# Attention over a key/value cache: tiles of four heads with 64 KiB rows, in three buffers that take turns

## The chip, the cores and the metric

The kernel runs on one core of one Trainium2 chip. The core has five engines with an instruction queue each: PE (TensorE, matrix products), DVE (VectorE), ACT (ScalarE), POOL (GpSimd) and SP (SyncE), which here issues nearly all loads. Loads go from the chip's HBM to SBUF, the on-chip memory of 128 partitions, through 16 DMA engines that all queues share. The metric is the time on the device in microseconds (us), the median of several runs.

## The reference, cut to what matters

One decode step of a transformer layer for two sequences: attention of one new token over a cache of 8192 keys and values, then a small gated network. All inputs are bf16.

```python
B, Sq, D = 2, 1, 512
Hq, Hkv, Sk, Dh = 32, 32, 8192, 128       # k_cache, v_cache: [B, Hkv, Sk, Dh]

def _A_ref(x, k, v, wq, wo):
    q = (x @ wq).reshape(B, Sq, Hq, Dh).transpose(0, 2, 1, 3)
    scores = einsum("bhqd,bhkd->bhqk", q, k) * (Dh ** -0.5)
    p = softmax(scores, axis=-1)
    o = einsum("bhqk,bhkd->bhqd", p, v)
    return o.transpose(0, 2, 1, 3).reshape(B, Sq, Hq * Dh) @ wo

def _B_ref(x, W_gate, W_up, W_down):      # F = 1376
    gate, up = x @ W_gate, x @ W_up
    return (gate * (gate > 0) * up) @ W_down

h = x + _A_ref(layernorm(x), ...)
out = h + _B_ref(layernorm(h), ...)
```

The two caches hold 2 x 2 x 32 x 8192 x 128 bf16 numbers, 268 MB, and each is read once. Each head has its own keys and values, so a key is used for one dot product and a value for one weighted sum.

## The kernel before, in words

**Tiles.** A tile is one sequence and two heads (`NG` = 16 pairs of heads, `steps` has N = 32 tiles). A tile's 2 x 8192 keys are spread over the 128 partitions: 64 partitions for each head (`HALF`), NT = 128 keys in each partition, so a partition's row is 128 x 128 bf16 = 32 KiB (`ROW`). One load of K or of V is 128 such rows, 4 MiB (`load_kv`, L140 to L148). K has two buffers (`kbuf`), V two (`vbuf`), tile i uses number i mod 2. The weights `wq` and later `wo` have a buffer of their own (`wbig`).

**Scores** (`scores`, L320). DVE multiplies the whole K tile by the tile's query in place (L358), the query being repeated over the keys (`qrep`). Then it halves each key's 128 products four times by adding one half to the other (L383: 64, 32, 16, 8 sums), and reduces the last 8 (L387) to the 128 scores of each partition, `scol`. In the last tile PE transposes 16 of the columns and multiplies them by q (L346, L337), and ACT sums 8 columns with its accumulator (L373).

**Softmax.** `pm` is each partition's maximum (L395). A PE product with a constant matrix brings the maxima of all partitions to every partition (`mx_ps`, L397). `powers` (L305) takes each head's extreme from that product on DVE (`nm`, L312), and ACT writes the exponentials to `pgz` (L315), one instruction for each head, with their sums in `zc`.

**Values** (`values`, L414). PE multiplies four columns of exponentials by four keys' values at a time. 32 such matmuls make a tile. Two stand by themselves (L408), 30 run in a hardware loop of two each on PE's sequencer (L438 to L440). The loop is in a block of its own (`tile_critical`, L434), which PE enters by semaphore waits and a branch (recorded at L642). ACT copies the result out (`collect`, L450). After each group of tiles `turn` and `sums` bring the outputs to columns, and `normalise` divides.

**Order of the work.** PE, DVE, ACT and SP run their instructions in the order in which the program lists them. In `scores(i)` the product of tile i comes first, then `powers(i-1)` and `values(i-1)`, then the loads of K(i+1) and V(i) are listed, then the halving of tile i and the PE product for its maximum. So the sequence of loads on SP is wq, K0 in four pieces, K1, V0, and then K(i+1), V(i) for each tile. The last tiles' values are not looped: FRONT of tile N-2 early, the last tile in columns (L420).

**The query** (`make_q`, L231). For each group of 512 columns of `wq`, PE multiplies x by them (L234, four matmuls), ACT copies the row to `qrow` (L238), PE replicates it over the partitions (L242, four matmuls) and ACT copies that to `qrep` (L246). There are eight such groups. Two are made before the first tile, the others one by one behind `scores(0)` to `scores(5)`.

**The end.** Behind the last V come 8.4 MB of weights (`wo`, gate, up, down), into `wbig` and K's first buffer. Then follow the product with `wo` (L535), the layer norm, and the gated network (L571, L604).

Of the kernel before, what the change touches and what calls it, by code (L numbers as in the profile page):

```python
# [23 lines left out]
def kernel(  # L24
# [20 lines left out]
    HALF = P // 2  # L45


    NT = 2 * Sk // P
    ROW = NT * Dh
    NG = Hq // 2  # L50
# [3 lines left out]
    NPE = 16  # L54
    NACT = (0, 8)
# [4 lines left out]
    AGAIN = 8  # L60
# [18 lines left out]

    assert Sq == 1 and Hkv == Hq and Dh == P and D == KC * P and Hq == 32 and B == 2  # L80
# [4 lines left out]
    small = ctx.enter_context(tc.tile_pool(name="small", bufs=2))  # L85
# [4 lines left out]
    pad = big.tile([P, 192], bf16)  # L90
# [3 lines left out]
    wbig = big.tile([P, max(KC * Hq * Dh, sum(rows) * D)], bf16)  # L94
    wd_r = big.tile([P, D], bf16)

    kh = [kbuf[:, s, :] for s in range(2)]
    wq_all = wbig[:, 0:KC * Hq * Dh]
    wq_sb = wq_all.rearrange("p (c n) -> p c n", c=KC)

    wgu = kbuf[:, 0, 0:2 * KC * F].rearrange("p (k c f) -> p k c f", k=2, c=KC)
    wd_sb = kbuf[:, 0, 2 * KC * F:2 * KC * F + FULL * D].rearrange("p (f n) -> p f n", f=FULL)

    qrep = consts.tile([P, B, NG, Dh], bf16)
    qrow = consts.tile([P, Hq * Dh], bf16)
    pgz = [consts.tile([P, NT * 2], bf16, name=f"pgz{s}") for s in range(2)]
    zc = consts.tile([P, B, NG, 2], f32)
# [8 lines left out]
    pick = consts.tile([P, B, HALF], bf16)  # L116
    sel = consts.tile([P, T4, 4, 2], f32)
# [6 lines left out]
    qT = consts.tile([P, 2, B], bf16)  # L124
    xrow = consts.tile([P, D], bf16)
    xc = consts.tile([P, B, KC], f32)
    hc = consts.tile([P, B, KC], f32)

    steps = [(b, g) for b in range(B) for g in range(NG)]
    N = len(steps)  # L130

    COLS = N - 1
    LOOPED = N - 3


    TOGETHER = N - 4

    FRONT = 24

    def load_kv(cache, buf, i, pieces=1):  # L140
        b, g = steps[i]
        w = ROW // pieces
        for k in range(pieces):
            nc.sync.dma_start(  # L144
                out=buf[i % 2][:, k * w:(k + 1) * w],
                in_=_dram(cache, (b * Hkv + 2 * g) * Sk * Dh + k * w, [[ROW, P], [1, w]]),
                single_packet=0 < i < TOGETHER,
            )  # L148

# [14 lines left out]
    with tc.manual_schedule(engines=ORDERED):  # L164

        nc.sync.dma_start(out=wq_all, in_=_dram(A_wq, 0, [[KC * Hq * Dh, P], [1, KC * Hq * Dh]]))  # L166
# [10 lines left out]
        select(pick, 1.0, 0, [[-1, B], [0, HALF]], 1)  # L177
# [3 lines left out]
        for s in range(2):  # L181
            nc.gpsimd.memset(pgz[s], 0.0)
# [14 lines left out]
        for j in range(2):  # L197
            select(sel[:, :, :, j], 1.0, -j, [[-2, T4], [-32, 4]], 1)
# [32 lines left out]
        def make_q(n):  # L231
# [7 lines left out]
            r_ps = ps2.tile([P, B, 2, Dh], f32, tag="tp", name="r_ps")  # L239
            for b in range(B):  # L240
                for j in range(2):
# [4 lines left out]
            nc.scalar.activation(out=qrep[:, :, 2 * n:2 * n + 2, :], in_=r_ps, func=ACT.Copy)  # L246
            if n == NG // 2 - 1:
                qT_ps = ps.tile([P, 2, B], f32, tag="acc")
                for h in range(2):
                    nc.tensor.matmul(  # L250
                        out=qT_ps[:, h, :], lhsT=qrow[0:B, (Hq - 2 + h) * Dh:(Hq - 1 + h) * Dh],
                        rhs=ident[0:B, 0:B], start=True, stop=True,
                    )
# [7 lines left out]
        groups = {}  # L261
        for b in range(B):
            for g0 in range(0, NG, 4):
                if b == B - 1 and g0 + 4 == NG:
                    for g1, n in ((g0, 3), (g0 + 3, 1)):
                        groups[b * NG + g1 + n - 1] = (b, g1, n)
                else:
                    groups[b * NG + g0 + 3] = (b, g0, 4)

        divided = {NG - 1: (0, 0, NG), N - 5: (1, 0, NG - 4), N - 2: groups[N - 2], N - 1: groups[N - 1]}  # L270
# [10 lines left out]
        def o_of(i):  # L281
            key = B if i == N - 1 else steps[i][0]
            if key not in o_ps:
                o_ps[key] = ps2.tile([P, 2, 2 * NG], f32, tag="o", name="o_ps")
            return o_ps[key]

        def sums(i):
            b, g0, n = groups[i]
            nc.tensor.matmul(  # L289
                out=o_of(i)[:, 1, 2 * g0:2 * (g0 + n)], lhsT=ones, rhs=zc[:, b, g0:g0 + n, :], start=True, stop=True,  # L290
            )

        def normalise(i):
            b, g0, n = divided[i]
            c = slice(2 * g0, 2 * (g0 + n))
            rz = small.tile([P, 2 * NG], f32, tag="rz")
# [6 lines left out]
        cols = {}  # L303

        def powers(i):  # L305
            b, g = steps[i]
            s = i % 2
            mx_ps, scol = mx.pop(i)
            if i % AGAIN == 0:
                cols["nm"] = small.tile([P, AGAIN, 2], f32, tag="nm", name="nm")  # L310
            nm = cols["nm"][:, i % AGAIN, :]
            nc.vector.tensor_reduce(out=nm, in_=mx_ps, axis=AXIS.X, op=ALU.min)  # L312
            for j in range(2):
                r = slice(j * HALF, (j + 1) * HALF)
                nc.scalar.activation(  # L315
                    out=_free(pgz[s][r, :], j, [[2, NT]]), in_=scol[r, :], func=ACT.Exp, scale=SCALE,
# [3 lines left out]
        def scores(i):  # L320
            b, g = steps[i]
            s = i % 2
            kt = kbuf[:, s, :]
            npe = NPE if i == N - 1 else 0
            nmul = NT - npe
            nv = nmul - NACT[i == N - 1]

            if i % AGAIN == 0:
                cols["scol"] = small.tile([P, AGAIN, NT], f32, tag="scol", name="scol")
            scol = cols["scol"][:, i % AGAIN, :]  # L330
            if npe:
                sc_ps = ps.tile([P, NPE, 2], f32, tag="sc")
                kT = small.tile([P, NPE * P], bf16, tag="kT")

                def times_q(c0):
                    for t in range(c0, c0 + TPC):
                        nc.tensor.matmul(  # L337
                            out=sc_ps[:, t, :], lhsT=kT[:, t * P:(t + 1) * P], rhs=_free(qT, b, [[B, 2]]),
                            start=True, stop=True,
                        )  # L340

                for c0 in range(0, NPE, TPC):
                    t_ps = ps2.tile([P, TPC, P], bf16, tag="tp")
# [3 lines left out]
                    nc.scalar.activation(  # L347
                        out=kT[:, c0 * P:(c0 + TPC) * P], in_=t_ps.rearrange("p t s -> p (t s)"), func=ACT.Copy,
                    )
                    if c0:  # L350
                        times_q(c0 - TPC)
                times_q(NPE - TPC)
                nc.scalar.activation(out=scol[0:HALF, nmul:NT], in_=sc_ps[0:HALF, :, 0], func=ACT.Copy)
                nc.scalar.activation(out=scol[HALF:P, nmul:NT], in_=sc_ps[HALF:P, :, 1], func=ACT.Copy)

            for t0, n in ([(0, NT // 2), (NT // 2, nmul - NT // 2)] if i == 0 else [(0, nmul)]):
# [19 lines left out]
            if i >= 1:  # L376
                if i < N - 1:
                    collect(i - 1)
# [17 lines left out]
            mx_ps = ps.tile([P, 2, HALF], f32, tag="mx")  # L396
# [5 lines left out]
            if 1 <= i < COLS:  # L402
                turn(i - 1)

        def products(i, u0, u1):
            s = i % 2
            for u in range(u0, u1):
                nc.tensor.matmul(  # L408
                    out=made[i][0:2 * T4, :], lhsT=pgz[s][:, u * 2 * T4:(u + 1) * 2 * T4],
                    rhs=vbuf[s][:, u * T4 * Dh:(u + 1) * T4 * Dh],  # L410
# [3 lines left out]
        def values(i):  # L414
            s = i % 2
            if i >= COLS:
                sums(i)
                g = steps[i][1]
                for t in range(NT):
                    nc.tensor.matmul(  # L420
                        out=o_of(i)[:, 0, 2 * g:2 * g + 2],
                        lhsT=vbuf[s][:, t * Dh:(t + 1) * Dh], rhs=pgz[s][:, 2 * t:2 * t + 2],
                        start=(t == 0), stop=(t == NT - 1),
                    )
                    if t == NT // 2:
                        turn(i - 1)
# [3 lines left out]
            if i >= LOOPED:  # L430
                products(i, 0, FRONT if i == N - 2 else NT // T4)
                return

            with tc.tile_critical(sync_engine=PE):  # L434
# [3 lines left out]
                with nc.Fori(1, NT // T4 // LOOP, 1, engines=[PE], head_slot=at) as w:  # L438
                    for u in range(LOOP):
                        nc.tensor.matmul(  # L440
                            out=made[i][0:2 * T4, :],
# [205 lines left out]
```

## Time and profile before

| | |
|---|---|
| median of 3 runs | 659.24 us (659.11 to 659.24) |
| the profiled execution, first to last instruction (its span) | 657.6 us |
| bytes read from HBM | 281.05 MB |
| DVE busy | 607.9 us (92%) |
| PE busy | 398.7 us (61%) |
| ACT busy | 67.0 us (10%) |
| load queue of SP, share of the DMA engines' time | 99.3% |
| loads of K and of V, 4 MiB each | 64, the first K in four pieces |

The profile is of one further execution. Its page gives the span and no other time for that execution; what a run has around the span is the difference of 1.6 us to the median. The page has the busy time of each engine, the same in 40 slices with the DMA rate, the queues, the chain of work that ended last, and groups of instructions by line. The trace behind the page can be asked for stretches, single instructions and waits. A name such as `kbuf<-kbuf,qrep` says what an instruction writes and reads. SPq and PEq are the sequencers of SP and PE: what they record are loads issued and semaphores waited for.

### The profile page before, as it was taken

The numbers are of one execution on the slowest core, as the hardware profiler recorded it, in microseconds if no ns is written. First come the engines' busy times: TensorE is split into PE (matmuls) and PEld (weight loads), VectorE is DVE, ScalarE is ACT, GpSimd is POOL, SyncE is SP. The second block draws the span as 40 slices with busy tenths as digits, with TensorE's granted clock in tenths as the row PEclk, the third lists the DMA queues.
The fourth block names the chain that finished last, engine by engine and source line by source line (L and its number), as shares of the span: only waits on it lengthen the run. The fifth ranks groups of instructions, "written<-read, shape, count | busy, mean of one in ns | idle before, by whom it ended". The sixth has DMA issues, their size and how long they took to land.

```text
span 657.6 us, 7128 instructions
## 1 busy us (share of the span) xinstructions
PE 398.7 (61%) x1647; PEld 129.5 (20%) x1647; DVE 607.9 (92%) x290; ACT 67.0 (10%) x200; POOL 7.9 (1%) x51
## 2 busy tenths in 40 slices
PE   2127666666676555657666556775556665565496
PEld 1002111211121111211112111121112111121256
DVE  0899999999999999999999999999999999999941
ACT  2110111110000000000000000000000000000220
POOL 4000000000000000000000000000000000000000
PEclk9999788798887777898887789767778876779885
DMA  8999999999999999999999999999999999999997
GB/s 359 439 444 421 442 433 427 444 415 446 427 434 433 427 442 425 440 434 427 440 424 441 429 435 432 429 440 424 440 431 432 438 423 441 432 433 436 425 422 298
DMA packets 11379, 281.26 MB, mean 428 GB/s; under 512 B 1282, under 2 KB 1380, under 8 KB 2020
## 3 DMA queue, kind: packets, MB, share of 16 engines
q1 hardware_dynamic: 11360, 281.06, 99.3%
q8 instruction: 9, 0.15, 0.1%
q14 instruction: 6, 0.05, 0.0%
q10 hardware_dynamic: 4, 0.00, 0.0%
HBM read 281.05 MB, written 0.00 MB: 427 GB/s over the span
## 4 chain that ended last, share of the span: by engine, by line
DVE 61%; DMA 36%; PE 1%; issue 1%; SPq 0%; ACT 0%; DVEq 0%; ACTq 0%
DMA kbuf<-in_A_k_cache_dram 30%; DVE kbuf L358 28%; DVE kbuf L383 27%; DVE scol L387 4%; DMA vbuf<-in_A_v_cache_dram 3%; DMA kbuf<-in_B_W_down_dram 3%; PE po L408 1%; DVE nm L312 1%; DVE pm L395 0%; SPq L144 0%; ACT pgz L315 0%; PE d_ps L604 0%; SPq L166 0%; DVE rz L297 0%; PE y_ps L612 0%
## 5 line engine op out<-in xcount | busy, mean ns | idle before, releaser
L440 PE MATMUL po<-vbuf,pgz 128*8 x870 | 300.1, 443 | 68.0 <-issue 66.7
L358 DVE TENSOR_TENSOR kbuf<-kbuf,qrep 128x16384 bf16<-128x16384 bf16 (+2 forms) x33 | 277.1, 8398 | 10.2 <-DMA kbuf<-in_A_k_cache_dram 9.8
L383 DVE TENSOR_TENSOR kbuf<-kbuf 128x8192 bf16<-128x8192 bf16 (+4 forms) x128 | 274.5, 2144 | 3.3
L440 PEld LDWEIGHTS po<-vbuf,pgz 128*8 x870 | 79.9, 92 | 299.1 <-issue 263.9
L408 PE MATMUL po<-vbuf,pgz 128*8 128x512 bf16 x122 | 47.0, 521 | 135.4 <-PEq L434 111.3
L450 ACT ACTIVATE ob<-po 8x512 f32<-8x512 f32 x31 | 18.2, 586 | 436.5 <-PEq L434 427.3
L387 DVE TENSOR_REDUCE scol<-kbuf 128x128 f32<-128x1024 bf16 (+1 forms) x32 | 38.8, 1214 | 1.2
L315 ACT ACTIVATE pgz<-scol,nm 64x128 bf16<-64x128 f32 x64 | 28.0, 438 | 85.4 <-DVE nm L312 84.5
L397 PE MATMUL mx_ps<-nscale,pm 128*128 128x128 f32 x64 | 15.0, 317 | 29.7 <-DVE pm L395 19.0
L408 PEld LDWEIGHTS po<-vbuf,pgz 128*8 128x8 bf16 x58 | 2.7, 84 | 130.4 <-issue 130.4
L397 PEld LDWEIGHTS mx_ps<-nscale,pm 128*128 128x128 f32 x64 | 9.7, 190 | 39.6 <-issue 19.3
L234 PE MATMUL q_ps<-wbig,xn 128*2 128x512 bf16 x32 | 10.7, 469 | 3.0 <-DMA wbig<-in_A_wq_dram 3.0
L315 ACT ACTIVATION_READ_ACCUMULATOR pgz<-scol,nm 64x1 f32 x64 | 11.7, 184 | 0.0
L312 DVE TENSOR_REDUCE nm<-mx_ps 128x2 f32<-128x128 f32 x32 | 9.1, 284 | 1.4 <-PE mx_ps L397 1.4
L408 PEld LDWEIGHTS <-pgz 128*8 128x8 bf16 x64 | 6.1, 98 | 21.3 <-ACT pgz L315 10.0
L395 DVE TENSOR_REDUCE pm<-scol 128x1 f32<-128x128 f32 x32 | 9.1, 286 | 1.1
L459 PE MATMUL o_ps<-sel,ob 128*128 128x8 f32 (+1 forms) x64 | 8.7, 262 | 0.1
L459 PEld LDWEIGHTS o_ps<-sel,ob 128*128 128x128 f32 x64 | 8.0, 197 | 1.4 <-ACT ob L450 1.2
L215 DVE COPY xc<-x_ps 128x8 f32<-128x8 f32 x1 | 0.2, 167 | 8.4 <-PE x_ps L211 8.4
L238 ACT ACTIVATE qrow<-q_ps 2x512 bf16<-2x512 f32 x8 | 4.7, 587 | 29.5 <-PE q_ps L234 29.5
L242 PE MATMUL r_ps<-qrow,pick 2*64 2x256 bf16 x32 | 3.9, 321 | 5.4 <-ACT qrow L238 5.4
L297 DVE RECIPROCAL rz<-o_ps 128x32 f32<-128x32 f32 (+3 forms) x4 | 1.0, 254 | 5.8 <-PE o_ps L289 4.6
(93 smaller groups left out, 75.5 us busy)
## 6 DMA issues: line engine op xcount, KB each, us to landing
vbuf<-in_A_v_cache_dram SPq DMA_DIRECT2D x32, 4096.0 KB, 23.4
kbuf<-in_A_k_cache_dram SPq DMA_DIRECT2D x31, 4096.0 KB, 19.8
wbig<-in_A_wq_dram SPq DMA_DIRECT2D x1, 4096.0 KB, 12.6
kbuf<-in_A_k_cache_dram SPq DMA_DIRECT2D x4, 1024.0 KB, 17.5
wbig<-in_A_wo_dram SPq DMA_DIRECT2D x1, 2048.0 KB, 24.5
wbig<-in_A_wo_dram SPq DMA_DIRECT2D x2, 1024.0 KB, 26.4
kbuf<-in_B_W_gate_dram SPq DMA_DIRECT2D x1, 1376.0 KB, 31.2
kbuf<-in_B_W_up_dram SPq DMA_DIRECT2D x1, 1376.0 KB
```

The lines of the kernel that those rows point to most:

```text
L234: nc.tensor.matmul(out=q_ps[0:B, :], lhsT=xn[:, c, :], rhs=wq_sb[:, c, n * 512:(n + 1) * 512], start=(c == 0), stop=(c == KC - 1),)
L312: nc.vector.tensor_reduce(out=nm, in_=mx_ps, axis=AXIS.X, op=ALU.min)
L315: nc.scalar.activation(out=_free(pgz[s][r, :], j, [[2, NT]]), in_=scol[r, :], func=ACT.Exp, scale=SCALE, bias=nm[r, j:j + 1], accum_out=zc ...
L358: nc.vector.tensor_tensor(out=kv, in0=kv, in1=_free(qrep, (b * NG + g) * Dh, [[0, n], [1, Dh]]), op=ALU.mult,)
L383: nc.vector.tensor_tensor(out=lo, in0=lo, in1=_free(kt, half, [[Dh, nv], [1, half]]), op=ALU.add,)
L387: nc.vector.tensor_reduce(out=scol[:, 0:nv], in_=_free(kt, 0, [[Dh, nv], [1, 8]]), axis=AXIS.X, op=ALU.add,)
L395: nc.vector.tensor_reduce(out=pm, in_=scol, axis=AXIS.X, op=ALU.max)
L397: nc.tensor.matmul(out=mx_ps.rearrange("p a b -> p (a b)"), lhsT=_free(pm, 0, [[0, P]]), rhs=nscale, start=True, stop=True,)
L408: nc.tensor.matmul(out=made[i][0:2 * T4, :], lhsT=pgz[s][:, u * 2 * T4:(u + 1) * 2 * T4], rhs=vbuf[s][:, u * T4 * Dh:(u + 1) * T4 * Dh], s ...
L440: nc.tensor.matmul(out=made[i][0:2 * T4, :], lhsT=pgz[s][:, bass.ds((w * LOOP + u) * (2 * T4), 2 * T4)], rhs=vbuf[s][:, bass.ds((w * LOOP ...
L450: nc.scalar.activation(out=ob[32 * k:32 * k + 2 * T4, :], in_=made.pop(i)[0:2 * T4, :], func=ACT.Copy,)
L459: nc.tensor.matmul(out=o_of(i)[:, 0, 2 * g0:2 * (g0 + n)], lhsT=ob[:, t * Dh:(t + 1) * Dh], rhs=sel[:, t, 0:n, :], start=(t == 0), stop=(t ...
```

## The change

- A tile is four heads (`H4`) and one sequence. Each head has 32 partitions (`QP`), each partition 256 keys (`NT`), a row is 64 KiB. There are 16 tiles, 16 loads of K and 16 of V of 8 MiB each. K's first load is in four pieces as before, now of 2 MiB, V's last in two.
- Three buffers `buf[0..2]` of 64 KiB for each partition take turns, for K and V alike. V(i) goes to the buffer in which K(i) was (`v_at`, `k_at`), when the scores of tile i are done. K(i+2) goes to the buffer of V(i-1), when that tile's values are done. At the start `wq`, `qrow` and `xrow` lie in `buf[1]`, where V0 goes next. At the end all the weights lie in the last K's buffer.
- The loads are listed after `scores(i)`: V(i), then K(i+2).
- One group of `make_q` is made before the first tile, the seven others behind `scores(0)`. The replication has eight matmuls, one for each sequence and head, of half the width.
- A tile has 64 matmuls of `values` in its loop block, and `powers` four exponentials. There is one `pgz`, one `scol`, one `nm`; the pool `small` has one buffer for each name in place of two.
- ACT sums 32 columns in tiles 0 and 1, 8 in the others, 16 in the last. PE makes 48 columns of the last tile's scores. Tiles 14 and 15 have their values in columns (`COLS`).
- `collect` and `turn` come a tile later, in front of and behind `powers(i-1)` of the next `scores`.
- The loads no longer ask for `single_packet`.

```diff
-    NT = 2 * Sk // P
+    H4 = 4
+    QP = P // H4
+    NT = H4 * Sk // P
...
-    NPE = 16
-    NACT = (0, 8)
+    NPE = 48
...
-    small = ctx.enter_context(tc.tile_pool(name="small", bufs=2))
+    small = ctx.enter_context(tc.tile_pool(name="small", bufs=1))
...
-    kbuf = big.tile([P, 2, ROW], bf16)
-    vbuf = [big.tile([P, ROW], bf16, name=f"vbuf{s}") for s in range(2)]
+    buf = [big.tile([P, ROW], bf16, name=f"buf{s}") for s in range(3)]
...
+    k_at = {i: (i - 2) % 3 if i else 0 for i in range(N)}
+    v_at = {i: k_at[i] if i else 1 for i in range(N)}
+    v_at[N - 1] = v_at[N - 3]
+
+    wq_sb = buf[1][:, 0:KC * Hq * Dh].rearrange("p (c n) -> p c n", c=KC)
+    qrow = buf[1][:, KC * Hq * Dh:KC * Hq * Dh + Hq * Dh]
+    xrow = buf[1][:, (KC + 1) * Hq * Dh:(KC + 1) * Hq * Dh + D]
...
+    tail = buf[k_at[N - 1]]
+    wo_sb = tail[:, 0:NWO]
+    wgu = tail[:, NWO:NWO + NGU].rearrange("p (k c f) -> p k c f", k=2, c=KC)
...
+    COLS = N - 2
+    NACT = {i: 32 if i < 2 else 16 if i == N - 1 else 8 for i in range(N)}
...
-                single_packet=0 < i < TOGETHER,
...
+    def load_k(i, pieces=1):
+        load_kv(A_k_cache, buf[k_at[i]], i, pieces)
+
+    def load_v(i, pieces=1):
+        load_kv(A_v_cache, buf[v_at[i]], i, pieces)
...
-        load_kv(A_k_cache, kh, 0, pieces=4)
-        load_kv(A_k_cache, kh, 1)
-        load_kv(A_v_cache, vbuf, 0)
+        load_k(0, pieces=4)
+        load_k(1)
...
             for b in range(B):
-                for j in range(2):
+                for j in range(H4):
                     nc.tensor.matmul(
-                        out=r_ps[j * HALF:(j + 1) * HALF, b], lhsT=pick[0:B, b, :],
-                        rhs=_free(qrow[0:B, :], (4 * n + j) * Dh, [[2 * Dh, 2], [1, Dh]]), start=True, stop=True,
+                        out=r_ps[j * QP:(j + 1) * QP, b], lhsT=pick[0:B, b, :],
+                        rhs=qrow[0:B, (H4 * n + j) * Dh:(H4 * n + j + 1) * Dh], start=True, stop=True,
                     )
...
-        EARLY = 2
-        for n in range(EARLY):
-            make_q(n)
+        make_q(0)
...
-            left = waiting[:]
+            if i >= 2:
+                collect(i - 2)
             if i >= 1:
                 powers(i - 1)
+            if i >= 2:
+                turn(i - 2)
+            left = waiting[:]
             if i >= 1:
                 values(i - 1)
                 tc.no_sync_barrier()
-                if i < N - 1:
-                    load_kv(A_k_cache, kh, i + 1)
-                    load_kv(A_v_cache, vbuf, i)
...
         for i in range(N - 1):
             scores(i)
-            if i + EARLY < NG // 2:
-                make_q(i + EARLY)
-
-        load_kv(A_v_cache, vbuf, N - 1)
+            if i == 0:
+                for n in range(1, NG):
+                    make_q(n)
+            load_v(i)
+            if i + 2 < N:
+                load_k(i + 2)
+        load_v(N - 1, pieces=2)
+        scores(N - 1)
...
-        scores(N - 1)
-        products(N - 2, FRONT, NT // T4)
+        turn(N - 2)
         powers(N - 1)
-        collect(N - 2)
+        normalise(N - 2)
         values(N - 1)
-        turn(N - 1)
-        while waiting:
-            normalise(waiting.pop(0))
+        normalise(N - 1)
```

More of the change, by code (lines that the diff above doesn't have):

```diff
@@ L59 @@
     PARTS = KC * KC
-    AGAIN = 8
     LOOP = 2
@@ L123, with load_kv @@
     orow = [consts.tile([P, n, B], bf16, name=f"orow{k}") for k, n in enumerate(rows)]
-    qT = consts.tile([P, 2, B], bf16)
-    xrow = consts.tile([P, D], bf16)
+    qT = consts.tile([P, H4, B], bf16)
+    kT = consts.tile([P, TPC * P], bf16)
     xc = consts.tile([P, B, KC], f32)
     hc = consts.tile([P, B, KC], f32)
[L129 to L140, printed above, removed]
+    COLS = N - 2
+    NACT = {i: 32 if i < 2 else 16 if i == N - 1 else 8 for i in range(N)}
+    def load_kv(cache, t, i, pieces=1):
         b, g = steps[i]
@@ L180 @@
         select(nscale, -SCALE, 0, [[-1, P]], 1)
-        for s in range(2):
-            nc.gpsimd.memset(pgz[s], 0.0)
+        nc.gpsimd.memset(pgz, 0.0)
         nc.gpsimd.memset(zc, 0.0)
@@ L254, in make_q @@
                 nc.scalar.activation(out=qT, in_=qT_ps, func=ACT.Copy)
-        EARLY = 2
-        for n in range(EARLY):
-            make_q(n)
[L261 to L270, printed above, removed]
+        make_q(0)
+        groups = {3: (0, 0, 4), 7: (0, 4, 4), 11: (1, 0, 4), 13: (1, 4, 2), 14: (1, 6, 1), 15: (1, 7, 1)}
+        assert NG == 8 and COLS == 14
+        divided = {NG - 1: (0, 0, NG), N - 3: (1, 0, NG - 2), N - 2: groups[N - 2], N - 1: groups[N - 1]}
         o_ps = {}
@@ L301 @@
         mx = {}
-        cols = {}
         def powers(i):
             b, g = steps[i]
-            s = i % 2
             mx_ps, scol = mx.pop(i)
-            if i % AGAIN == 0:
-                cols["nm"] = small.tile([P, AGAIN, 2], f32, tag="nm", name="nm")
-            nm = cols["nm"][:, i % AGAIN, :]
+            nm = small.tile([P, H4], f32, tag="nm")
             nc.vector.tensor_reduce(out=nm, in_=mx_ps, axis=AXIS.X, op=ALU.min)
-            for j in range(2):
-                r = slice(j * HALF, (j + 1) * HALF)
+            for j in range(H4):
+                r = slice(j * QP, (j + 1) * QP)
                 nc.scalar.activation(
-                    out=_free(pgz[s][r, :], j, [[2, NT]]), in_=scol[r, :], func=ACT.Exp, scale=SCALE,
+                    out=_free(pgz[r, :], j, [[H4, NT]]), in_=scol[r, :], func=ACT.Exp, scale=SCALE,
                     bias=nm[r, j:j + 1], accum_out=zc[r, b, g, j:j + 1],
@@ L321, in scores, with transposed @@
             b, g = steps[i]
-            s = i % 2
-            kt = kbuf[:, s, :]
+            kt = buf[k_at[i]]
             npe = NPE if i == N - 1 else 0
             nmul = NT - npe
[L326 to L330, printed above, removed]
+            nv = nmul - NACT[i]
+            scol = small.tile([P, NT], f32, tag="scol")
             if npe:
[L332 to L343, printed above, removed]
+                sc_ps = ps.tile([P, NPE, H4], f32, tag="sc")
+                def transposed(c0):
+                    t_ps = ps2.tile([P, TPC, P], bf16, tag="tp", name="t_ps")
                     for k in range(TPC):
@@ L375, in scores @@
                 )
-            if i >= 1:
-                if i < N - 1:
-                    collect(i - 1)
+            if npe:
+                for j in range(H4):
+                    r = slice(j * QP, (j + 1) * QP)
+                    nc.scalar.activation(out=scol[r, nmul:NT], in_=sc_ps[r, :, j], func=ACT.Copy)
             width = Dh
@@ L516 @@
             for b in range(B):
-                sp = small.tile([P, P], bf16, tag="spread")
+                sp = kT[:, b * P:(b + 1) * P]
                 if blocks is not WHOLE:
```

120 lines of the change are left out of this document (59 added, 61 removed).

## The prediction, made before the result was known

> **What bounds the kernel now.** I read the page's DMA rows and chain first, then the stages, then single waits.
>
> ```profile
> span 657.6 us, 7128 instructions
> ...
> PE 398.7 (61%) x1647; PEld 129.5 (20%) x1647; DVE 607.9 (92%) x290; ACT 67.0 (10%) x200; POOL 7.9 (1%) x51
> ...
> q1 hardware_dynamic: 11360, 281.06, 99.3%
> ...
> DVE 61%; DMA 36%; PE 1%; issue 1%; SPq 0%; ACT 0%; DVEq 0%; ACTq 0%
> ```
> The chain names DVE first, yet the load queue is busy for 99.3% of the span. The stages settle it (columns: engines' busy time, granted clock, DMA share, GB/s):
>
> ```profile
> 100.00:200.00 100.00, 65.84 (x221) 20.12 (x220) 99.15 (x43) 12.98 (x37) 0.00 (x0) 0.84 1.00 431
> ...
> 400.00:500.00 100.00, 62.27 (x187) 18.22 (x188) 97.38 (x44) 7.85 (x25) 0.00 (x0) 0.80 1.00 433
> 500.00:600.00 100.00, 62.88 (x198) 18.99 (x197) 98.13 (x43) 7.85 (x25) 0.00 (x0) 0.81 1.00 433
> ```
> The rate is flat at about 433 GB/s. 281.06 MB at 433 take 649 us of the 657.6, so DMA bounds the kernel. DVE follows closely behind it. Any gap in the load stream is lost for good. Hence the question is what the new buffers make each load wait for. Two things in the old trace price it: the set-up of q, and how PE enters its loop over V.
>
> ```profile
> 0.81 0.39 SPq L166 DMA_DIRECT2D wbig<-in_A_wq_dram  x1
> ...
> 13.45 1.86 PE L234 MATMUL q_ps<-wbig,xn 128*2 128x512 bf16 x4 [2.97 <-DMA wbig<-in_A_wq_dram]
> ...
> 18.41 4.42 DVE L358 TENSOR_TENSOR kbuf<-kbuf,qrep 128x8192 bf16<-128x8192 bf16 x1 [5.65 <-DMA kbuf<-in_A_k_cache_dram]
> ...
> 49.03 1.01 PE L408 MATMUL po<-vbuf,pgz 128*8 128x512 bf16 x2 [7.02 <-PEq L434]
> ...
> 62.88 0.33 SPq L144 DMA_DIRECT2D vbuf<-in_A_v_cache_dram  x1
> ```
> ```profile
> L642 PEldq EVENT_SEMAPHORE  x176: 51/51/51, 48.1 to 657.6; - x176
> L642 PEldq COMPARE_BRANCH  x29: 169/169/302, 48.8 to 587.2; - x29
> ```
> The second fence gives durations in ns (minimum, median, maximum). Before each of the 29 loops PE's sequencer passes six semaphore waits and a branch. All took 51 ns, so whatever they waited for had always arrived. The list of the built program's instructions says what that is: every semaphore at the count it has at that place in the program, every load issued so far included.
>
> **The change part by part.** All times below are on the trace's own clock. A load on an idle queue: wq was issued at 0.81 and used at 13.45. Its 4 MiB take 9.69 us at 433, so 2.95 us are fixed. 8 MiB take 19.37 us. K0 to K15 and V0 to V15 name the tiles' loads.
>
> Bytes, rate and traffic: unchanged; larger rows cannot beat a flat rate, and I find no reason for a loss, so 0. The lost `single_packet` likewise: K0 without it came at 2 MiB per 4.83 us (18.41 to 23.24), 434 GB/s.
>
> Start. In both kernels wq, K0 and K1 stream without a gap. K1's last byte comes 16 MiB (38.7 us) after wq's, about 51.3. The next load, V0, goes into the buffer that holds wq and qrow, so it must wait for the last `make_q`. The seven later `make_q` now stand on PE behind tile 0's maximum. K0's four 2 MiB pieces: DVE starts the fourth at 18.41 + 3 x 4.84 = 32.93 and ends it at 37.35. The four halving passes and the reduction took 10.0 us for 128 columns (27.70 to 37.68); 224 columns scale to 17.5, less about 0.7 of fixed parts, so 16.8: 54.15. Maximum 0.4, the PE product and its hand-over 0.85 (37.72 to 38.84, less the shorter maximum): the first of the seven starts at 55.4. A cold `make_q` runs 1.86 (matmuls), 0.59 (copy), 0.05 twice for hand-overs, and the replication, which was 0.56 to the next one with four matmuls; eight half as long lie between 0.56 and 1.12, and I take 0.65, since the four column groups overlap as the two did. That is 3.2 each. A warm one (63.45 to 65.15, plus replication) is 2.3. Cold is nearer, as PE idles before. 55.4 + 7 x 3.2 + 0.4 (the qT products) = 78.2: V0 issued, usable at 78.2 + 2.95 + 19.37 = 100.5. K2, behind it on SP's queue, is usable at 119.9. The queue idles for about 29 us. ACT's 32 column sums on K0 (0.30 each alone, perhaps 0.5 with one scratch tile) end by 54 at the latest and cost nothing; the cover is DVE's 17 us.
>
> The Trainium skill, TensorE: Matmul & The Clock Gate, Part 1, has PE at full clock after about 3.4 us of sustained work. By it six of the seven groups would be warm and V0 would come 5.4 us sooner. The row from 13.45 to 18.41, where two groups ran cold for 5 us, speaks against it.
>
> Steady state. SP's order is V0, K2, V1, K3, V2, K4 and so on. The loop over V(i-1) stands in tile i, after K(i+1) was issued, so its entry waits for K(i+1) as well, which it does not read. K(i+2) overwrites V(i-1) and waits for this loop's end. So K(i+1)'s landing, the loop, K(i+2)'s load follow each other:
> - Entry after the landing: six waits 0.106 apart and the branch need 1.0 (48.02 to 49.03 in the old trace). K's own wait is one among them, so 0.3 to 0.9; I take 0.55.
> - The loop: 32 matmuls took 13.57 to 13.85 from the first to SP's issue behind it (49.03 to 62.88, 68.29 to 81.86). 32 more are 16 pairs at 0.885 (54.97, 55.88, 56.74). 13.57 + 14.16 = 27.7; bounds 27.2 to 28.4.
> - Fixed part of a load on an idle queue 2.95. The lower end is the 1.3 us from issue to landing of the 2 KB output. Above, the x rows took 7.3 us behind wq, which nothing does here; 3.5 is the end I keep. Nearest in kind is wq.
> - 19.37.
>
> The sum is 50.57 us per tile of 38.74 us of traffic. The rest hides in this. DVE: 17.22 for the product (8.69 plus 8.53 by the step from 4.42 to 8.69), then `nm`, which needs the PE product behind the loop, so it waits until 0.55 + 27.7 + 0.85 after the landing. With 18.45 (10.0 x 1.94 less 0.9) and 0.3, V(i+1) is issued 47.9 after the landing, 2.7 before K(i+2) is in, and follows without a gap. V has 9.7 us more before SP's next K could start; beyond that lateness costs fully. ACT's exponentials (four for two) and eight sums run beside DVE's halving.
>
> 13 periods from K2 put K15 at 119.9 + 657.4 = 777.3, and the loop over V13 ends at 805.6.
>
> The Trainium skill, DMA: Bandwidth & Descriptors, Anatomy of one DMA, gives a load 2.0 us fixed plus its bytes at 436 GB/s, measured there on another issue path: 21.2 for 8 MiB in place of 22.3. By that the forecast would be 843, 15 lower. wq's row here shows about 1 us more.
>
> End. V15 waits for that loop. The remaining PE and ACT chain: product 0.85; six rounds of transposes and copies 8.5 (two took 3.1); copy and four exponentials 3.2; 256 matmuls on V14, 8 (65 took 1.79); DVE's and ACT's last sums 1.2; maximum and product 0.85, exponentials 2.95, 256 matmuls on V15, 7.5. That is 33.0, to 838.6. Then as before from 639.35 to 652.70, 13.3, to 851.9; the last matmuls 1.4; from there to the span's end 2.9: 856.2. Weights behind V15 land at 805.6 + 2.95 + 19.4 + 19.4 = 847.4, hidden. The runs' median stands 1.64 above the profiled span: **857.8**.
>
> **The rivals.**
> A: the loop starts at V's own landing, and PE's entry waits are passed in time. For it: they all took 51 ns in the trace. Against: then no load issued ahead of them was later than V. DVE's 17.22 + 0.2 + 18.45, plus 2 us of hand-overs, are under the 38.74 of traffic, so only the start remains: 657.6 + 29 + 1.6 = 688.
> B, the other side: DVE is the bound, as the chain's 61% has it. Its work falls to about 577 us (no halving for the 32 + 32 + 13 x 8 + 16 columns that ACT sums, no product either for 48 of the last tile, half the small instructions), and 659 - 31 = 628. It decides only if loads pass 281 MB in 622 us, 452 GB/s, never idle; no 100 us stage exceeds 433.
> C: loads that restart on an idle queue, or 64 KiB rows, come in slower. 1% costs 0.19 us on a K load, 2.5 in all; 10% gives 883.
>
> **How the numbers follow.** The forecast has 0.86, A 0.08, C beyond my range 0.04, B 0.01; 0.01 is left for no change. The terms' ends, taken as independent, give the forecast -23 and +14: loop -7 and +10, fixed part -22 (the smallest transfer, unlikely in full) and +8, entry -4 and +5, start -6 and +3. I keep 837 to 876, some nine parts in ten of the forecast. A change of 0.2% is about what a measurement here can tell. Slower 0.98, same 0.01, faster 0.01.
>
> **What would show it.** DMA idle from about 51 to 80 us; K landings 50.6 us apart; PE loops of 27.5 us that start within 1 us of a K landing; semaphore waits at the loop's entry of many us; SP waiting for the loop's end before K; DVE waiting some 11 us per tile for the product behind the loop; mean 330 GB/s. V0 issued before 60 refutes the start. Loops that start 19 us before K lands refute the period, and leave A.

## The result, and the profile after

The changed kernel takes **863.82 us** (median of 4 runs, 863.15 to 869.13) against 659.23 (659.11 to 659.24): a ratio of 1.312, 95% interval 1.309 to 1.316. The forecast was 857.8, in a range of 837 to 876. The profiled execution took 863.65 and has a span of 861.9.

First the page's lines on the span, the engines, the rate in 40 slices and the load queue of the changed kernel:

```profile
span 861.9 us, 7740 instructions
...
PE 366.9 (43%) x1963; PEld 126.8 (15%) x1963; DVE 574.5 (67%) x164; ACT 155.1 (18%) x541; POOL 8.5 (1%) x52
...
GB/s 384 443 146 195 438 438 195 435 246 380 398 243 409 225 432 249 380 398 232 401 231 401 292 389 389 243 411 125 436 344 244 435 198 438 243 389 389 243 414 130
...
q1 hardware_dynamic: 6896, 281.06, 77.0%
```

The bytes are the same 281.06 MB and a slice that is full still runs at 432 to 443 GB/s. The time went to the slices at 125 to 300: the load queue was busy for 77.0% of the span, and for 99.3% before. DVE has 574.5 us of work, 33 fewer than before, and it did not help.

Next the waits, of the engines and of SP's queue (who waited, for whom: us in all, how often, the longest), and then the waits by which PE's sequencer enters the loops (ns: minimum, median, maximum):

```profile
PE po L393 <- DMA buf<-in_A_k_cache_dram: 325.0, 14, 42.2
...
DVE nm L302 <- PE mx_ps L384: 174.4, 15, 16.7
```
```profile
SPq L144 <- PEq L413: 449.5, 14, 48.3
```
```profile
L625 PEldq EVENT_SEMAPHORE  x86: 51/51/19097, 98.0 to 861.9; - x86
```

Each of the 14 loops over V waited for a load of K, though it reads only V; SP then waited 14 times for such a loop. At the entries of four loops a wait of 17 to 19 us is on record, where none had been over 51 ns before. In front of the other ten the records say 51 ns too, and only PE's idle time of some 22 us shows the wait. One period, from the rows of SP, and of DVE and PE (start, duration):

```profile
145.91 0.33 SPq L144 DMA_DIRECT2D buf<-in_A_k_cache_dram  x1
...
165.25 0.33 SPq L144 DMA_DIRECT2D buf<-in_A_v_cache_dram  x1
...
196.57 0.33 SPq L144 DMA_DIRECT2D buf<-in_A_k_cache_dram  x1
```
```profile
168.19 17.23 DVE L343 TENSOR_TENSOR buf<-buf,qrep 128x32768 bf16<-128x32768 bf16 x1 [2.49 <-DMA buf<-in_A_k_cache_dram]
...
168.85 1.02 PE L393 MATMUL po<-buf,pgz 128*16 128x512 bf16 x2 [22.46 <-DMA buf<-in_A_k_cache_dram]
...
219.04 1.02 PE L393 MATMUL po<-buf,pgz 128*16 128x512 bf16 x2 [21.83 <-DMA buf<-in_A_k_cache_dram]
```

K is issued at 145.91 and is there at 168.19, when DVE starts its product. The loop starts at 168.85, 22.94 behind the issue, runs 27.5, and the next K goes out at 196.57. V, issued at 165.25, moves inside the loop and is done long before it ends; then the queue is empty. The circle comes round every 50.4 us for 38.74 us of traffic.

The start, as rows of PE and SP: the first of the seven groups of q, the last one's closing product, and V0 behind it.

```profile
55.40 1.86 PE L237 MATMUL q_ps<-buf,xn 128*2 128x512 bf16 x4
...
75.49 0.26 PE L253 MATMUL qT_ps<-ident,buf 2*128 2x2 bf16 x4
```
```profile
75.82 0.33 SPq L144 DMA_DIRECT2D buf<-in_A_v_cache_dram  x1
```

Between 51 and 78 the load queue had almost nothing to do (39 GB/s).

### The profile page after: what moved, and what is told of

The parts are those of the page before. It is cut to its first block, busy times and chain, and to the rows that moved or that the text cites. A ratio compares the mean times of both kernels' runs of the same rounds, so it can differ in the third digit from the quotient of the medians.

```text
span 861.9 us, 7740 instructions
## 1 busy us (share of the span) xinstructions
PE 366.9 (43%) x1963; PEld 126.8 (15%) x1963; DVE 574.5 (67%) x164; ACT 155.1 (18%) x541; POOL 8.5 (1%) x52
## 3 DMA queue, kind: packets, MB, share of 16 engines
q1 hardware_dynamic: 6896, 281.06, 77.0%
## 5 line engine op out<-in xcount | busy, mean ns | idle before, releaser
L419 PE MATMUL po<-buf,pgz 128*16 x868 | 290.6, 411 | 88.3 <-issue 86.5
L343 DVE TENSOR_TENSOR buf<-buf,qrep 128x32768 bf16<-128x32768 bf16 (+2 forms) x19 | 272.9, 14362 | 61.0 <-DMA buf<-in_A_k_cache_dram 56.7
L370 DVE TENSOR_TENSOR buf<-buf 128x15872 bf16<-128x15872 bf16 (+5 forms) x64 | 251.5, 3929 | 1.7
L419 PEld LDWEIGHTS po<-buf,pgz 128*16 x868 | 78.9, 91 | 305.5 <-issue 268.1
L302 DVE TENSOR_REDUCE nm<-mx_ps 128x4 f32<-128x128 f32 x16 | 4.7, 291 | 174.4 <-PE mx_ps L384 174.4
L359 ACT ACTIVATE whole<-buf 128x128 f32<-128x128 bf16 x184 | 56.9, 309 | 26.5 <-DVE buf L343 20.7
L305 ACT ACTIVATE pgz<-scol,nm 32x256 bf16<-32x256 f32 x64 | 55.1, 861 | 11.6 <-DVE nm L302 6.1
L374 DVE TENSOR_REDUCE scol<-buf 128x248 f32<-128x1984 bf16 (+2 forms) x16 | 34.7, 2166 | 1.9 <-ACT pgz L305 0.4
L359 ACT ACTIVATION_READ_ACCUMULATOR whole<-buf 128x1 f32 x184 | 34.2, 186 | 0.0
L237 PE MATMUL q_ps<-buf,xn 128*2 128x512 bf16 x32 | 14.9, 621 | 2.8 <-DMA buf<-in_A_wq_dram 2.8
L305 ACT ACTIVATION_READ_ACCUMULATOR pgz<-scol,nm 32x1 f32 x64 | 16.0, 249 | 0.0
L384 PEld LDWEIGHTS mx_ps<-nscale,pm 128*128 128x128 f32 x32 | 5.2, 203 | 48.9 <-issue 39.3
## 6 DMA issues: line engine op xcount, KB each, us to landing
buf<-in_A_k_cache_dram SPq DMA_DIRECT2D x4, 2048.0 KB, 23.5
```

Source lines behind the costliest of these rows:

```text
L237: nc.tensor.matmul(out=q_ps[0:B, :], lhsT=xn[:, c, :], rhs=wq_sb[:, c, n * 512:(n + 1) * 512], start=(c == 0), stop=(c == KC - 1),)
L305: nc.scalar.activation(out=_free(pgz[r, :], j, [[H4, NT]]), in_=scol[r, :], func=ACT.Exp, scale=SCALE, bias=nm[r, j:j + 1], accum_out=zc[r ...
L343: nc.vector.tensor_tensor(out=kv, in0=kv, in1=_free(qrep, (b * NG + g) * Dh, [[0, n], [1, Dh]]), op=ALU.mult,)
L359: nc.scalar.activation(out=whole, in_=kt[:, t * Dh:(t + 1) * Dh], func=ACT.Copy, accum_out=scol[:, t:t + 1],)
L370: nc.vector.tensor_tensor(out=lo, in0=lo, in1=_free(kt, half, [[Dh, nv], [1, half]]), op=ALU.add,)
L374: nc.vector.tensor_reduce(out=scol[:, 0:nv], in_=_free(kt, 0, [[Dh, nv], [1, 8]]), axis=AXIS.X, op=ALU.add,)
```

## The experiments

The theory: two costs, nearly independent. The seven groups of q behind tile 0 hold V0 back by some 25 us; and the loop's entry waits for a load that it does not need, on which the next load in turn waits. Rivals: the restarts or the 64 KiB rows are slow in themselves, or DVE is the bound.

**Listing K behind the loop.** `load_k(i + 1)` moves from the end of tile i-1's turn to the place behind `values(i - 1)`. The instructions of PE and SP and their order stay the same; only the counts for which the loop's entry waits change.

```diff
                 values(i - 1)
                 tc.no_sync_barrier()
+                if i + 1 < N:
+                    load_k(i + 1)
...
             load_v(i)
-            if i + 2 < N:
-                load_k(i + 2)
```

> The changed kernel, with one line moved: K(i+1) is listed behind the loop over V(i-1) in the program, not ahead of it. SP issues the same loads in the same order, PE, DVE and ACT run the same instructions in the same order; only the counts for which PE waits at the loop's entry change. Theory (the entry waits for K(i+1), and so landing, loop and next load stand in a row): loops start at V's landing, the period falls from the measured 50.4 us to the 38.7 us of traffic, the loss at the start (V0 issued at 75.8) stays, the end stays some 5 us longer than forecast; 690 us. Rival 1 (three buffers are too few, K(i+2) waits for the loop over V(i-1) and that alone makes the period) and rival 2 (the loop on PE is too slow): nothing moves, 864 us.

Measured: 700.37 us (699.03 to 701.72), ratio to before 1.0625 (1.0602 to 1.0649). A loop of this run, and DVE's next product, which starts when K(i+1) is there:

```profile
178.22 1.02 PE L395 MATMUL po<-buf,pgz 128*16 128x512 bf16 x2 [10.49 <-ACT whole L361]
```
```profile
195.65 17.22 DVE L343 TENSOR_TENSOR buf<-buf,qrep 128x32768 bf16<-128x32768 bf16 x1 [3.06 <-DMA buf<-in_A_k_cache_dram]
```

The loop starts 17.4 us ahead of K's arrival, and no longer 0.7 behind it. The loops start 39.6 us apart on average, and 163.5 us are gone. So the wait for K(i+1) carries four fifths of the loss. It ended 10 us above the 690 expected: a tile took 39.6 and not 38.74. The third and fifth experiments go into that.

**The groups of q ahead of tile 0.** All eight are made before the first scores; the entry waits stay.

```diff
-        make_q(0)
+        for n in range(NG):
+            make_q(n)
...
-            if i == 0:
-                for n in range(1, NG):
-                    make_q(n)
```

> The changed kernel, with all eight make_q ahead of tile 0's scores, the rest untouched. Theory (V0 waits for the last make_q, which waits behind tile 0's maximum): the eight end near 13.2 + 8 x 2.9 = 36, before K1's last byte at 51.3, V0 follows K1 without a gap, K2 is in 26 us earlier (about 91 in place of 117), the period stays 50.4: 864 - 26 = 838 us. Rival (the gap at the start is hidden by the first loops, or V0 waits for something else of tile 0): 864 us, V0 still issued after 54.

Measured: 838.57 us (838.10 to 839.04), ratio 1.2722 (1.2696 to 1.2747), 25.3 us less than the changed kernel. V0 in this run:

```profile
36.63 0.33 SPq L144 DMA_DIRECT2D buf<-in_A_v_cache_dram  x1
```

V0 goes out at 36.63 instead of 75.82. The period stays at 50.4.

**Both at once.** The two edits above together.

> Both edits at once: K listed behind the loop, all make_q first. Theory (the two waits are independent and are all of the loss up to the end of the loops): 690 - 26 = 664 us, the queue never idle before the last K, 433 GB/s in every stage with the 64 KiB rows, DVE with about 1 us to spare in each tile. Rival 1 (DVE's 35.9 us and the hand-overs of a load do not fit into 38.7 us): each us over is 13 us more, 677 us at one. Rival 2 (loads with rows of 64 KiB move slower): 1% is 6.5 us more, and the stages show it.

Measured: 676.25 us (673.27 to 679.23), ratio 1.0244 (1.0215 to 1.0274). The gains add up (163.5 + 25.3 = 188.8; together 187.6). The two causes carry 187.6 of the 204.6 us that the change costs, 92%; 17 remain. A tile takes 39.8 us, 1.06 more than its traffic, and 13 such tiles are 14 of the 17. The expected 664 is missed; its first rival, 677 for one microsecond over in each tile, is what came. The load queue around the issue of V (169.96), and between two such places (columns: stretch, its length, busy time of the engines, granted clock, DMA share, GB/s):

```profile
168.00:173.00 5.00, 3.69 (x12) 0.95 (x12) 2.31 (x2) 0.00 (x0) 0.00 (x0) 1.00 0.62 223
174.00:198.00 24.00, 10.16 (x31) 2.98 (x32) 24.00 (x3) 7.25 (x25) 0.00 (x0) 0.79 1.00 431
```

Where the queue has work, 64 KiB rows come at 431 GB/s, as 32 KiB rows did. The rate falls only where V is issued, behind DVE's last reduction of the tile: V follows K into the same buffer, and DVE's 35.9 us plus the hand-overs (3.9 on average, from DVE's last reduction of a tile to its next product) are no longer under the 38.74.

**Four products per pass of the loop.** Everything of the changed kernel stays, but the loop is shorter.

```diff
-    LOOP = 2
+    LOOP = 4
```

> The changed kernel, with four matmuls in each turn of PE's loop in place of two; the entry's waits stay. Theory (landing, loop and next load in a row): whatever the loop of 64 matmuls saves against its 27.5 us, the period saves too, 14 times. By the gap of 0.25 us behind each pair, if it comes once in four matmuls, the loop takes about 21 us and the whole 864 - 14 x 6.5 = 773 us. Rival (the period is set by the loads' restart or by DVE, the loop only lies beside it): the loop shortens, the time stays at 864 us.

Measured: 768.07 us (768.06 to 768.09), ratio 1.1652 (1.1629 to 1.1676). Two issues of K behind two loops in this run:

```profile
183.21 0.33 SPq L144 DMA_DIRECT2D buf<-in_A_k_cache_dram  x1
...
227.14 0.33 SPq L144 DMA_DIRECT2D buf<-in_A_k_cache_dram  x1
```

The loops take 20.8 us instead of 27.5, and the loops start 43.7 apart on average. In the changed kernel it is 50.4, without its one long tile. What the loop loses (6.7) the period loses: the loop is a term of the circle, in full. PE is busy 43% of the changed kernel's span, and still each microsecond of its loop counts. The time lies 5 us under the expected 773, mainly because the tenth loop, 4.8 us longer than the others in the changed kernel (see below), is like the others here.

**Less work for DVE.** To the run with both edits, one more: ACT sums 24 columns instead of 8 in tiles 2 to 14.

```diff
-    NACT = {i: 32 if i < 2 else 16 if i == N - 1 else 8 for i in range(N)}
+    NACT = {i: 32 if i < 2 else 16 if i == N - 1 else 24 for i in range(N)}
```

> The kernel with both causes taken out (all eight groups of q ahead of the first scores, K(i+1) listed behind the loop over V(i-1); 676.25 us), and in tiles 2 to 14 ScalarE sums 24 columns of the scores instead of 8, so VectorE has 16 columns fewer to add up. Theory: that kernel ran 39.8 us per tile instead of the 38.74 of its traffic because V is issued behind VectorE's last reduction, about 1 us after the queue has nothing else to move; 16 columns fewer of 256 take about 16/248 of the 17 us of VectorE's reduction, 1.1 us, so V is issued 1.1 us sooner, the tile is back near 38.74 and 13 tiles times 1.06 us are saved: 662 us (660 to 665). Rival: rows of 64 KiB, or going from one queue entry to the next, cost the 1 us themselves: then the tile stays at 39.8 and the time at 676 (674 to 678). Second rival: ScalarE's 16 more sums of about 0.43 us, 6.9 us per tile, end later than VectorE and V waits for them: slower than 676.

Measured: 670.84 us (668.55 to 672.50), ratio 1.0165 (1.0146 to 1.0183). Neither theory's number. DVE's tile is 34.76 us instead of 35.89, as planned, but the tile comes down from 39.8 to 39.3 only. Around the issue of V (168.16), and over most of the tiles:

```profile
167.00:171.00 4.00, 2.82 (x9) 0.77 (x9) 1.52 (x2) 0.00 (x0) 0.00 (x0) 1.00 0.78 262
...
115.00:586.00 471.00, 267.88 (x822) 76.59 (x822) 418.91 (x99) 163.28 (x680) 0.00 (x0) 0.84 1.00 428
```

The dip is smaller but there. V's late issue makes up about half of the microsecond, since the tile moved with it by 0.5 us; that rows or restarts cost the whole of it is refuted. The other half is not idle time. From 115 to 586 the DMA engines are busy throughout (share 1.00) and move 428 GB/s, where the kernel before moved 433 at the same share: 0.45 us for the bytes of a tile. In the trace it is packets behind an issue that take longer: 4% of the 64 KiB packets take over a tenth more than the usual 2.42 us, and most of these begin within 5 us behind the issue of a load. So this half fits the first rival, a cost of going from one queue entry to the next. Why such packets are slow, and whether a still earlier issue would end it, was not tested. The size of the rows is not the reason: a run with rows of 32 KiB, further down, has it too. The second rival fell: in tiles 2 to 14 ACT's last sum ends 3.3 us ahead of DVE's reduction.

**Another place for the tenth loop.** The changed kernel's tenth loop takes 32.3 us, the others 27.5 to 27.8. It is the tenth loop, and no other, in every run with two products per pass that leaves its place, at 571 us in one run and at 429 in another. PE's rows, of the changed kernel first (two products a row, duration second):

```profile
577.61 0.80 PE L419 MATMUL po<-buf,pgz 128*16 x2 [0.24 <-issue]
578.65 0.80 PE L419 MATMUL po<-buf,pgz 128*16 x2 [0.24 <-issue]
...
804.06 0.63 PE L419 MATMUL po<-buf,pgz 128*16 x2 [0.28 <-issue]
804.92 0.63 PE L419 MATMUL po<-buf,pgz 128*16 x2 [0.24 <-issue]
```

A pass takes 1.04 us there and 0.86 to 0.90 elsewhere, the clock being granted in full at both places. Nor does the clock set the pace: in the first 3 to 5 us of the other loops it is granted at 0.5, and a pass takes 0.82 to 0.85 there. The edit pads PE's stream so that the tenth loop's code begins at a set slot, as the first one's does:

```diff
-                at = {PE: LOOP_AT} if i == 0 else None
+                at = {PE: LOOP_AT if i == 0 else 64} if i in (0, 9) else None
```

> The changed kernel with one edit: the code of the 10th loop over V is put at a set place (as the first one's is already), its instructions and their order are the same. Theory: that loop took 32.3 us instead of 27.5 in every run of this code with two products per pass, because of where its few instructions lie in PE's stream; moved, it takes 27.5, and as each tile's loop lies on the path the run is 4.8 us shorter: 859 us (858 to 860). Rival: it is the data or the moment (clock, transfers beside it) of that tile: unchanged, 864.

Measured: 859.86 us (858.91 to 863.90), ratio 1.3058 (1.3022 to 1.3095). The tenth loop now takes 28.1, its passes as here:

```profile
578.15 0.63 PE L419 MATMUL po<-buf,pgz 128*16 x2 [0.30 <-issue]
579.03 0.63 PE L419 MATMUL po<-buf,pgz 128*16 x2 [0.24 <-issue]
```

Same instructions, same data, nearly the same moment and the same granted clock: it is the place of the code that costs 4.2 us there. The times of the two kernels touch at their ends (863.15 and 863.90), so the length of the loop itself is the evidence. That the slow place is a boundary between two blocks of instructions is likely, but was not shown.

**The entry wait alone, in the kernel before.** There the load of K(i+1) moves ahead of the loop in the program, as the change has it; tiles and buffers stay as they were.

```diff
             if i >= 1:
+                if i < N - 1:
+                    load_kv(A_k_cache, kh, i + 1)
                 values(i - 1)
                 tc.no_sync_barrier()
                 if i < N - 1:
-                    load_kv(A_k_cache, kh, i + 1)
                     load_kv(A_v_cache, vbuf, i)
```

> The kernel before with one part of the change: the load of K(i+1) is listed ahead of the loop over V(i-1) instead of behind it, so that the loop's entry waits for K(i+1) there too. Theory: the entry wait alone is not what costs; it costs where the next load of K also waits for that loop's end. Here K and V have two buffers each, K(i+2) waits for VectorE only. The loop starts about 8 us later (324.2 where the trace has 316.1), ends at 337.6, and still frees V's buffer before the queue needs it (about 342). What is late is nm: VectorE has its product ready at 333.1 and would wait till about 338, and over two tiles the circle is issue and landing of K 13.7, loop and hand-over 14.2, maximum and nm 1, reduction 10.3: 39.2 against 38.7 of traffic. So 0.2 to 0.5 us per tile, 664 (660 to 670). Rival: the entry wait costs its delay in each tile wherever it stands: 659 + 14 x 8 = 771.

Measured: 676.25 us (674.97 to 679.26), ratio 1.0275 (1.0241 to 1.0309). The expectation counted 14 loops, as the changed kernel has; this one has 29, of half the size. With that count its own prices, 0.2 to 0.5 us a tile, make 665 to 674, and the rival's 659 + 29 x 8 = 891. Measured are 17.2 us, 0.59 a tile, still 2 us above these prices. Waits, load queue and a long stretch of this run:

```profile
PE po L409 <- DMA kbuf<-in_A_k_cache_dram: 84.2, 16, 11.0
...
DVE nm L312 <- PE mx_ps L398: 21.0, 18, 4.0
```
```profile
q1 hardware_dynamic: 11360, 281.06, 98.3%
```
```profile
100.00:600.00 500.00, 307.54 (x949) 89.69 (x948) 477.90 (x203) 42.78 (x132) 0.00 (x0) 0.81 1.00 424
```

The loops do wait for K here, and now DVE waits for the maximum behind the loop, 21.0 us in 18 waits, which it did once before, for 1.4 us. But the load queue keeps 98.3%: with buffers of their own for K and V, no load waits for a loop in such a way that the queue runs dry. Most of the 17 us shows as slower flow, 424 GB/s in place of 433 at the same share of 1.00, here with rows of 32 KiB. The entry wait becomes dear only where the next load waits for that loop's end.

**Half the products of the last two tiles.** Every second product of V14 and V15 is left out, so half of their V is missing from the result.

```diff
-                for t in range(NT):
+                for t in range(0, NT, 2):
```

> The changed kernel without every second product over V of the last two tiles (half of their V is left out of the result): 256 of 512 products of about 28.5 ns go from the unrolled stretches of the tail, 7.3 us. Theory: the stops of 2.62 and 1.78 us within these stretches, at which PE waited for nothing that the trace shows, are PE waiting for its instructions (blocks of 16 KB land beside them); 256 products fewer are 512 instructions, two such blocks fewer behind the last loop, and at most one of the two stops stays: 863.8 - 7.3 - 1.8 to 4.4 = 852 to 855. Rival: the stops belong to the data (V's two pieces, the weights) and stay as they are, 2.6 and 1.8 us: 856.5.

Measured: 854.90 us (853.90 to 859.02), ratio 1.2989 (1.2948 to 1.3031). PE's rows in the tail of the changed kernel, with the three stops for which it has no releaser:

```profile
828.14 1.82 PE L405 MATMUL o_ps<-pgz,buf 128*128 128x4 bf16 x63 [2.62 <-issue]
...
843.12 1.95 PE L405 MATMUL o_ps<-pgz,buf 128*128 128x4 bf16 x67 [1.78 <-issue]
...
849.55 2.47 PE L518 MATMUL att_ps<-orow,buf 128*128 128x2 bf16 x70 [1.03 <-issue]
```

and in the run with half the products:

```profile
820.38 3.55 PE L405 MATMUL o_ps<-pgz,buf 128*128 128x4 bf16 x128
...
833.34 3.55 PE L405 MATMUL o_ps<-pgz,buf 128*128 128x4 bf16 x128
...
838.28 4.46 PE L518 MATMUL att_ps<-orow,buf 128*128 128x2 bf16 x128 [0.31 <-DVE orow L512]
```

All three stops are gone, the one in the product with `wo` too, of which nothing was changed. From the issue of V15 behind the last loop to the span's end it is 46.8 us instead of 56.2, 9.4 less, where the missing products alone are 7.1. That is less than the 7.1 and 5.4 of the stops together, because in the first stretch another wait is next: DVE's maximum, which stood behind a reciprocal that needs these products, then waits for ACT's last copies of scores and comes only 2.8 us sooner. So the stops go with the code ahead of them and not with the data. The run with four products per pass, whose code is longer ahead of the tail, says the same: its stops stand behind other products, and two of them are 128 products apart, which with their weight loads are 256 instructions:

```profile
743.74 3.58 PE L405 MATMUL o_ps<-pgz,buf 128*128 128x4 bf16 x128 [2.77 <-issue]
749.93 0.72 PE L405 MATMUL o_ps<-pgz,buf 128*128 128x4 bf16 x21 [2.62 <-issue]
```

In the changed kernel blocks of 16 KB begin on the queue for instructions at 825.6, 832.0, 840.8, 846.9, 850.7 and 855.2, two more behind the last loop than in this run, and PE goes on 1.3 to 1.6 us behind the end of the first, the third and the fourth. That PE waits for its instructions there fits all of this, though no record names it.

## Why the prediction was right, and where it was off

**The period** was right in its mechanism and its size: 50.57 forecast, 50.4 measured. The listing experiment takes the wait away and with it 163.5 us, and the experiment with four products per pass shows the loop as a term of the circle. By terms: from the loop's first product to the next issue of K 27.7, as forecast; from that issue to the next loop 22.65 on average (22.3 to 23.5; the period shown has 22.94), where 22.87 was summed from entry, fixed part and traffic. How that divides was a little different: K's landing is signalled 21.9 us behind its issue in the median, 2.5 more than the 19.37 of the bytes, and some 0.7 follow to the loop, where 2.95 and 0.55 had been taken. The Trainium skill, DMA: Bandwidth & Descriptors, Anatomy of one DMA, gives 2.0 us for the fixed part on another issue path; with it the sum would have been some 0.9 too small, with wq's row it was 0.2 too large, so taking the row was nearer. DVE waits 11.6 us a tile for `nm` (174.4 in 15), some 11 forecast, and that is hidden.

One reading behind it was weaker than it looked. The 51 ns before each loop of the old trace do not show that everything had arrived: the changed kernel has such records in front of ten loops for which PE stood idle for some 22 us. What carried the forecast was the list of the built program's instructions.

**The start** was right in its mechanism; the size was off by 2.4 us. The first of the seven groups starts at 55.40, to the hundredth as summed. The groups follow each other in 2.87 us and not 3.2: the eight replications took 0.40 and the next group began 0.33 behind their start, where 0.65 was taken. The first product of all seven stayed at 1.86 to 1.87 (a warm one of the old trace, at 63.45, took 1.02), so the choice of the cold duration held. By the Trainium skill, TensorE: Matmul & The Clock Gate, Part 1, as the forecast read it, six would have been warm. PE was busy for 15.6 of the 20.4 us from 55.40 to 75.80, but in pieces of some 2 us between ACT's copies; that these pieces are the reason was not tested.

**13 periods** from K2's landing were forecast at 657.4. They took 660.2: 2.0 less by the shorter period, and 4.8 more by the tenth loop, of which nothing in the forecast spoke. Steps that cancel, and that is luck: V15, issued behind the last loop, went out at 805.76, where 805.6 was forecast, although the start was 2.5 us sooner. A sum that comes out right at such a point is not yet evidence for its terms.

**The end** is the part that was wrong: 56.2 us from there, 50.6 forecast. "256 matmuls on V14, 8" and "256 matmuls on V15, 7.5" took 10.2 (819.79 to 829.96) and 9.4 (835.71 to 845.07), with the short product of the sums ahead of each. That is 4.0 of the 5.6, and 4.4 are the two stops in them. The forecast had scaled 65 products in a row of the old trace, in which no such stop falls. The steps ahead of these stretches took 2.2 more than forecast, 14.0 for 12.55 and 5.75 for 5.0, most of it in the exponentials of rows of 256, 0.87 each: the last group of four, forecast at 2.95, took 3.5. All that follows V15's products took 16.9, where 17.6 was forecast, although the third stop, of 1.03, lies in it.

**The rivals.** A, loops that start at V's landing, fell: only the run with K listed later looks like it, and that one at 700 and not 688, since DVE's 35.9 us were not "under the 38.74" once the hand-overs are 3.7 us, as in that run, instead of the 2 that A allowed. In the changed kernel the circle hid that. B fell at once: DVE's work is 574.5 us, 577 forecast, and bounds nothing. C, slow rows or restarts, fell as a cause of the 204.6: full stretches run at 431 to 443 GB/s, and K lands about as fast as forecast. The slow packets behind an issue, a per cent or two where loads are issued late, are what is left of it.

Range and median: the 6 us between 857.8 and 863.8 are the end's 5.6, and half a microsecond in all the rest, in which larger steps cancel.

## What to carry to other kernels

The hardware loop in a block of its own waited here at its entry for the loads listed ahead of it, not only for what it reads: look at what the program lists there. Such a wait costs little while each load has a buffer that does not depend on the loop (17 us of 676 here); with a buffer that K and V share it closes a circle of load, loop and load, and then every term of that circle counts in full, on an engine that is busy 43% (163.5 us of 864 here). Larger loads in fewer buffers gained nothing where the rate was flat already, and the issue of each has to come earlier by the whole hand-over, here some 4 us.

## What the hardware showed that was not expected

- The same loop of two products ran at 1.04 us per pass in one place of the code and at 0.86 to 0.90 in all others, at the same granted clock, and 4.2 us per 62 products went when only its place was changed (32.3 to 28.1).
- Long straight stretches of small products, 28 ns each, stop now and then for 1.0 to 2.6 us beside the landing of a block of instructions; in the run with four products per pass, three stops of 2.3 to 2.8. The Trainium skill, Runtime: NRT & Kernel Launch, Instruction fetch mechanics, has instructions come in blocks of 16 KiB ahead of need, with the fetch hidden by the pace of issue; at this pace the trace shows it not hidden, if these stops are it.
- A load queue that is busy throughout can still lose a per cent or two. In the run with 24 columns on ACT, V was issued some 4.6 us ahead of DVE's next product, and the queue moved 428 GB/s at a share of 1.00; in the kernel before with K listed ahead of the loop 424; in the kernel before itself 433.
